# A planned attention and MoE kernel: the first job's scores moved behind half of its gate spreads, and other margins in the planner

## The chip, the cores and the metric

The kernel runs on one core of one Trainium2 chip. The metric is the device time of one execution in microseconds; the times before are the median of three runs. A profile is one execution recorded by the hardware profiler; it has a span (first to last instruction) and a time of its own.

## What is computed

Three stages follow each other. The first is a gated linear attention in the manner of an mLSTM (4 batches, 8 heads, 768 steps, head size 40), which the reference writes as a loop over time:

```python
m_new = np.maximum(f_gate[:, :, t] + m, i_gate[:, :, t])
f_stab = np.exp(f_gate[:, :, t] + m - m_new)
i_stab = np.exp(i_gate[:, :, t] - m_new)
C = f_stab[..., None, None] * C + i_stab[..., None, None] * np.einsum('bhd,bhe->bhde', vt, kt)
n = f_stab[:, :, None] * n + i_stab[:, :, None] * kt
h_tilde = np.einsum('bhde,bhe->bhd', C, qt)
denom = np.maximum(np.abs(np.einsum('bhd,bhd->bh', n, qt)[:, :, None]), 1.0)
y[:, :, t] = sigmoid(o_gate[:, :, t]) * h_tilde / denom
```

Its output, 3072 tokens of 320 numbers, goes through two layers of the form `g(x @ w_in) @ w_out` with 2048 inner features: `g(h) = h - tanh(h)` in the first, and in the second `h` above 1, 0 below -1 and `(h + 1)**2 / 4` between.

## The kernel before

The time axis is cut into 6 chunks of 128 steps. A **job** is one chunk of one batch, 24 in all (`job`, line 408). Four jobs make a **block** of 512 tokens, and each of the two layers runs over 6 blocks and, in a block, over 16 slices `f` of 128 inner features: `step` computes `h = x @ w_in` (lines 651 and 661), `activate` the function on ScalarE (ACT) and VectorE (DVE), `second` adds `gh @ w_out` into four PSUM banks `a` (line 713), two slices later (`LAG`). In the first layer the jobs of block k+1 are threaded between the slices of block k.

A job goes this way. The gates' decays are spread over partitions: for the first four jobs by matmuls against columns of the identity (`t_f`, line 453, two halves of four heads, each in its own `h` bank), later by loads `fb` from DRAM. DVE scans them into `d` (line 462), once for each half. TensorE makes the scores `t_s` (line 475, later 493 with split inputs from line 490), DVE multiplies them into `d` (line 497), TensorE makes `t_n` (lines 524, 533), then follow ACT line 540, DVE lines 541 and 542, GpSimd (POOL) line 556, DVE line 558 (the product `x`), and the transposes `t_x` (line 562). From these ACT and DVE make the split inputs of the next block (lines 612 to 617). The state update is `t_c` (line 569) with ACT lines 577, 581 and DVE line 586. The gates themselves come from `gates` (line 342): exponentials on ACT (line 369), then transposes `t_i` on TensorE (line 374).

Beside that the weights, which come as 64-bit floats, are loaded, converted on ACT and DVE (`conv64`, lines 322 to 326) and split (`split_w`, line 335). Results of a block of the first layer are transposed on DVE (line 724) and stored to `xr_d` by four DMAs. All loads and stores but one stand in SyncE's queue (SP), line 287, which issues them in order.

The order of all this isn't written by hand. `Plan` (line 76) records every operation with an engine, an estimated duration and a priority, simulates the engines, and emits each engine's instructions in the order of the planned starts. A result counts as available `NEAR` ns after its end for another engine, `FAR` for TensorE, and an own `margin` later where one is set. The priority of job `n` of a later block is `st = NF * (k - 1) + NF * (n - BLK0[k]) / BLK[k] - AHEAD`, in units of slices, and its loads have `st - LOADS`. Up to the end of the first slice TensorE's planned gaps are filled with matmuls on zeros (`filler`, line 804), a whole number of them for each gap, plus `P.more[o]` ahead of an operation `o`.

Of the kernel before, what the change touches and what calls it, by code (L numbers as in the profile page):

```python
# [18 lines left out]
L = 128  # L19
# [23 lines left out]

LOAD = [-90, -89, -88, -86]
JOB0, JOBD, JOBS = -30, 4, 1.0
AHEAD, LOADS = 6, 3
GROUPS = [(0, 2)] + [(c, c + 1) for c in range(2, NC)]
GATES = [-95, 12, 28, 44, 58]
DECAYS = [-94, 13, 29, 45, 59]
# [26 lines left out]
class Plan:  # L76
# [1 line left out]

    NEAR, FAR, PE_OUT = 60.0, 130.0, 170.0
    DMA_IN, DMA_OUT, DMA_ISSUE = 1400.0, 900.0, 370.0
    BACKLOG = 4000.0
    PATIENCE = 150.0
    FILL, HEAD, COLD = 0.75, 1.0, 4000.0

    def __init__(self):
        self.ops, self.tags, self.last, self.read = [], {}, {}, {}
        self.warm, self.end_warm, self.filler, self.gate, self.more = True, None, None, None, {}

    def buf(self, pool, shape, dtype, tag, name, cap=1):
        b = Buf(pool, shape, dtype, tag, name, cap)
# [4 lines left out]
    def op(self, eng, ns, prio, fn, r=(), w=(), out=None, lock=False):  # L97
        o = Op()
        o.eng, o.ns, o.prio, o.fn, o.seq, o.out = eng, ns, prio, fn, len(self.ops), out
        o.allocs, o.preds, o.succs = [], set(), []  # L100
        o.bufs, o.fill, o.lock, o.margin = [], 0, lock, 0.0
        key = lambda x: x if isinstance(x, tuple) else (x, None)

        for x in map(key, r):
            if x in self.last:
                o.preds.add(self.last[x])
            self.read.setdefault(x, []).append(o)
        for x in map(key, w):
            if x in self.last:
                o.preds.add(self.last[x])  # L110
            o.preds.update(self.read.pop(x, ()))
            self.last[x] = o
        o.preds.discard(o)
        for b in {key(x)[0] for x in (*r, *w)}:
            if isinstance(b, Buf):
                b.users.append(o)
                o.bufs.append(b)
        if any(b.place[0].startswith("late_") for b in o.bufs):
            o.preds.add(self.gate)
        self.ops.append(o)  # L120
        return o

    def schedule(self):
# [32 lines left out]
        while done < len(self.ops):  # L156
# [24 lines left out]
            if o.out is not None:  # L181
                dma = max(dma, t + self.DMA_IN) + o.out
                o.end = dma + self.DMA_OUT + o.margin
                free[o.eng] = t + self.DMA_ISSUE
            else:
                free[o.eng] = t + o.ns
                o.end = t + o.ns + (self.PE_OUT if o.eng == "PE" else 0.0)
            for b in o.bufs:
                b.left -= 1
                b.end = max(b.end, o.end)  # L190
# [2 lines left out]
            for s in o.succs:  # L193
# [5 lines left out]
                if not s.left:  # L199
                    ready[s.eng].append(s)  # L200
            done += 1
        self.ops.sort(key=lambda o: (o.start, o.seq))

    def issue(self):
# [28 lines left out]
def mlstm_moe_moe(ctx: ExitStack, tc: tile.TileContext, ig, fg, qk, qk3, q3, nat, w1, w2, cst, out):  # L233
# [64 lines left out]
    def load64(layer, f, prio):  # L298
# [3 lines left out]
        else:  # L302
            t = abuf("w64", [128, 8 * WC], U8, 2)
        raw_w[layer, f] = t
        load(prio, lambda: t[:, 0:8 * WC - 3], lambda: (w1, w2)[layer][f].bitcast(U8)[:, 3:8 * WC],
             704, w=[t], rows=5629, margin=6000.0 if layer else 0.0)

    def conv64(layer, f, prio):

# [98 lines left out]
    def job(n, at, ld):  # L408
# [10 lines left out]
            for u in range(2):  # L419
                load(ld, lambda u=u: qs[u].t, lambda u=u: qk3[b, c - STACK // B, u], 480, w=[qs[u]])  # L420
        nt = wbuf(3, [128, 2 * DM + H * E1], F32, "nat0") if n == 0 else abuf("nat", [128, 2 * DM + H * E1], F32, 3)
        load(ld, lambda: nt.t, lambda: nat[b, c * L:(c + 1) * L], 484, w=[(nt, 0), (nt, 1), (nt, 2)], rows=3872, margin=1200 if n >= 8 else 0.0)
        kc = group[c]
        f = {}
        if n >= FIRST:
            for u in range(2):
                ft = abuf("fb", [128, HU, L], F32, 2)
                load(ld + 0.5, lambda ft=ft: ft.t.rearrange("p h t -> p (h t)"), lambda u=u: fr_d[
                    c, b * H + u * HU:b * H + (u + 1) * HU].rearrange("h t -> (h t)").unsqueeze(0).to_broadcast([128, HU * L]),
                    256, r=[("fr_d", kc)], w=[ft], rows=512, margin=1200 if n >= 8 else 0.0)  # L430
                f[u] = lambda ft=ft: ft.t.rearrange("p h t -> p (h t)"), ft
        if c > 0:
            g = abuf("gb", [120, 3, L], F32, 2)
            for i in range(3):
                m = 3 if i < 2 else 2
                load(ld + 0.7, lambda i=i, m=m: g[i * D:(i + 1) * D, 0:m, :], lambda i=i, m=m: gr_d[
                    c, b * H:(b + 1) * H].unsqueeze(0)[:, i:H:3].to_broadcast([D, m, L]),
                    20 * m, r=[("gr_d", kc)], w=[(g, i)], rows=512, margin=1200 if n >= 8 else 0.0)
            G = [(g, i) for i in range(3)]
            q = abuf("q3", [120, 3, L], F32, 1)  # L440
            load(ld + 0.8, lambda: q.t, lambda: q3[b, c], 180, w=[(q, 0), (q, 1)], rows=1536, margin=1200 if n >= 8 else 0.0)


        dk = {}
        d0 = wbuf(6 + n % 2, [128, 1024], F32, "d0") if n < FIRST else None
        wc = abuf("wc", [128, H], F32, 2)
        for u in range(2):
            p = at(0) if u == 0 else at(1)
            if n < FIRST:
                ft = jbank(n, "f", "t_f")  # L450
                for h in range(HU):
                    r = b * H + u * HU + h
                    op("PE", 2 * pe(L, 128, 2), p, lambda h=h, r=r, ft=ft: nc.tensor.matmul(  # L453
                        ft[:, h * L:(h + 1) * L], ident[:, r:r + 1].to_broadcast([128, 128]),
                        gt[0][0][:, 0:L], start=True, stop=True), [(gt[0][0], 0), (gt[0][0], "z", 32), (gt[0][0], "z", 64), "cs"], [ft])
                f[u] = lambda ft=ft: ft.t, ft
            if d0 is None:
                d = abuf("d", [128, 512], F32, 3)
# [19 lines left out]

        if n < STACK:
            o = op("PE", 455 + 2 * HU * 111, at(1), scores, [(qt, 0), (qt, 1)], [sp[0], sp[1]])  # L480
            if n == 1:
                P.more[o] = 3
        else:
# [460 lines left out]
```

## Time and profile before

| | us |
|---|---|
| three runs | 808.71, 808.29, 806.84 |
| median | 808.29 |
| profiled execution, own time | 807.17 |
| its span | 805.4 |
| TensorE busy in the span | 798.4 |
| DVE, ACT, POOL busy | 566.4, 426.3, 145.1 |

The granted TensorE clock is 1.0 of full speed in all 40 slices of the page. A timeline row gives the start, the length, the engine, the line, the operation and what it writes and reads, the shape and the count; in brackets stands the engine's idle time ahead of it and what ended it. Ends of matmuls are modelled, so a short wait can hide in the length of the matmul before it. `PE` is TensorE, and `SPq` the queue of SyncE.

### The profile page before, as it was taken

The numbers are of one execution on the slowest core, as the hardware profiler recorded it, in microseconds if no ns is written. First come the engines' busy times: TensorE is split into PE (matmuls) and PEld (weight loads), VectorE is DVE, ScalarE is ACT, GpSimd is POOL, SyncE is SP. The second block draws the span as 40 slices with busy tenths as digits, with TensorE's granted clock in tenths as the row PEclk, the third lists the DMA queues.
The fourth block names the chain that finished last, engine by engine and source line by source line (L and its number), as shares of the span: only waits on it lengthen the run. The fifth ranks groups of instructions, "written<-read, shape, count | busy, mean of one in ns | idle before, by whom it ended". The sixth has DMA issues, their size and how long they took to land.

```text
span 805.4 us, 15259 instructions
## 1 busy us (share of the span) xinstructions
PE 798.4 (99%) x6029; PEld 693.3 (86%) x6029; DVE 566.4 (70%) x924; ACT 426.3 (53%) x810; POOL 145.1 (18%) x146
## 2 busy tenths in 40 slices
PE   9999999999999999999999999999999999999998
PEld 7666888888988989898899898888889889898887
DVE  7999998988887897887466674645546465564644
ACT  4966876566586657554455543534435344342533
POOL 3142233213225234332100200200200101000000
PEclk9999999999999999999999999999999999999999
DMA  8979356676668576771543310100100000000000
GB/s 281 326 225 308 104 178 178 180 246 188 174 172 260 163 213 165 228 217 64 145 133 91 93 34 1 40 33 1 47 26 1 33 1 1 33 1 1 34 1 33
DMA packets 47619, 93.66 MB, mean 116 GB/s; under 512 B 4700, under 2 KB 25020, under 8 KB 47548
## 3 DMA queue, kind: packets, MB, share of 16 engines
q1 hardware_dynamic: 47500, 92.66, 38.8%
q8 instruction: 47, 0.77, 0.4%
q14 instruction: 24, 0.20, 0.1%
q10 hardware_dynamic: 48, 0.03, 0.0%
HBM read 78.88 MB, written 13.80 MB: 115 GB/s over the span
## 4 chain that ended last, share of the span: by engine, by line
PE 95%; DVE 2%; DMA 1%; SPq 0%; issue 0%; ACT 0%; POOL 0%; POOLq 0%; DVEq 0%; ACTq 0%
PE a L713 41%; PE h L661 38%; PE h L651 3%; PE t_n L533 2%; PE h L640 2%; PE t_n L524 2%; PE t_s L475 1%; PE t_c L569 1%; PE t_s L493 1%; PE t_x L562 1%; PE t_f L453 1%; PE spare L807 1%; DMA nat<-in_nat_dram 1%; DVE d L462 1%; SPq L287 0%
## 5 line engine op out<-in xcount | busy, mean ns | idle before, releaser
L661 PE MATMUL h<-x,w 128*128 128x512 f32 x1376 | 340.6, 396 | 0.0
L713 PE MATMUL a<-w,gh 128*128 128x320 f32 x1472 | 328.4, 310 | 0.0
L661 PEld LDWEIGHTS h<-x,w 128*128 128x128 f32 x1376 | 251.6, 188 | 55.2 <-issue 6.9
L713 PEld LDWEIGHTS a<-w,gh 128*128 128x128 f32 x1472 | 248.7, 188 | 8.0 <-ACT ob L736 1.8
L713 PE MATMUL a<-w,gl 128*128 128x320 f32 x736 | 228.2, 311 | 0.0
L684 DVE TENSOR_SCALAR g<-h 128x512 f32<-128x512 f32 x96 | 63.6, 684 | 115.9 <-PE h L661 115.9
L686 ACT ACTIVATE g<-g,half 128x512 f32<-128x512 f32 x96 | 66.9, 721 | 136.2 <-DVE g L684 135.7
L713 PEld LDWEIGHTS a<-w,gl 128*128 128x128 f32 x736 | 138.1, 188 | 0.4
L688 DVE TENSOR_TENSOR g<-h,g 128x512 f32<-128x512 f32 x96 | 64.6, 692 | 27.7 <-ACT g L686 26.9
L692 ACT CAST gh<-g 128x512 fp32r<-128x512 f32 x96 | 59.5, 623 | 43.1 <-DVE g L688 39.8
L680 DVE TENSOR_TENSOR h<-h,g 128x512 f32<-128x512 f32 x88 | 60.9, 693 | 26.8 <-ACT g L679 26.3
L679 ACT ACTIVATE g<-h 128x512 f32<-128x512 f32 x88 | 52.6, 598 | 46.6 <-PE h L661 46.2
L693 DVE TENSOR_TENSOR gl<-h,gh 128x512 fp32r<-128x512 f32 x88 | 59.9, 684 | 20.1 <-ACT gh L692 19.1
L777 POOL TENSOR_TENSOR x<-xl,x 128x512 fp32r<-128x512 f32 x18 | 24.8, 1398 | 271.2 <-ACT x L768 270.7
L692 ACT CAST gh<-h 128x512 fp32r<-128x512 f32 x88 | 51.4, 585 | 40.5 <-DVE h L680 25.4
L693 DVE TENSOR_TENSOR gl<-g,gh 128x512 fp32r<-128x512 f32 x96 | 61.9, 686 | 2.9
L462 DVE TENSOR_TENSOR_SCAN d<-fb,scan_id 128x512 f32<-128x512 f32 x40 | 52.8, 1326 | 2.0 <-DMA fb<-fr_d 1.8
L490 POOL TENSOR_TENSOR xf<-qkraw,xf 120x1024 fp32r<-120x1024 f32 x12 | 29.6, 2467 | 79.5 <-ACT xf L488 48.3
L488 ACT ACTIVATE xf<-qkraw,cs 120x512 fp32r<-120x512 f32 x48 | 32.7, 718 | 15.7 <-PE t_s L493 10.7
L497 DVE TENSOR_TENSOR d<-t_s,d 128x512 f32<-128x512 f32 x48 | 31.8, 680 | 4.6 <-PE t_s L493 2.4
L556 POOL TENSOR_TENSOR nat<-nat,dn 128x320 f32<-128x320 f32 x23 | 21.7, 944 | 69.6 <-DVE dn L542 67.7
L322 ACT ACTIVATE cvb<-w,half 128x704 bf16<-128x704 int8 x32 | 29.8, 932 | 2.1 <-DVE w L324 2.1
(105 smaller groups left out, 754.0 us busy)
## 6 DMA issues: line engine op xcount, KB each, us to landing
w<-in_w_dram SPq DMA_DIRECT2D x32, 703.6 KB
nat<-in_nat_dram SPq DMA_DIRECT2D x24, 484.0 KB
qkraw<-in_qk_dram SPq DMA_DIRECT2D x24, 480.0 KB
fb<-fr_d SPq DMA_DIRECT2D x40, 256.0 KB
w_d<-w SPq DMA_DIRECT2D x16, 352.0 KB
w<-w_d SPq DMA_DIRECT2D x16, 352.0 KB
qkraw<-in_qk_dram SPq DMA_DIRECT2D x24, 160.0 KB
xr_d<-xo SPq DMA_DIRECT2D x24, 160.0 KB
```

The source lines that it names most:

```text
L462: op("DVE", dve(1024), p, lambda o=dk[u][0], i=f[u][0]: nc.vector.tensor_tensor_scan(out=o(), data0=i(), data1=scan_id, initial=0.0, op0=A ...
L488: op("ACT", act(512, 1), at(u - 1), lambda raw=raw, t=t, z=z, cols=cols: nc.scalar.activation(t[:, cols], raw[:, cols], AF.Copy, scale=cs[ ...
L497: op("DVE", dve(512), at(2 + u), lambda p=sp[u], d=dk[u][0]: nc.vector.tensor_tensor(out=d(), in0=p.t, in1=d(), op=ALU.mult), [sp[u], dk[u ...
L661: op("PE", pe(n), prio, lambda i=i, c=c, s=s: nc.tensor.matmul(p[:, :n], w[:, c:c + 128], x[:, s, :n], start=(i == 0 and not layer), stop= ...
L679: op("ACT", act(n), prio + 0.5 - FFN, lambda: nc.scalar.activation(t[:, :n], p[:, :n], AF.Tanh), [p], [t])
L680: op("DVE", dve(n), prio + 0.5 - FFN, lambda: nc.vector.tensor_tensor(out=p[:, :n], in0=p[:, :n], in1=t[:, :n], op=ALU.subtract), [p, t], [p])
L684: op("DVE", dve(n), prio + 0.5 - FFN, lambda: nc.vector.tensor_scalar(t[:, :n], p[:, :n], -1.0, 1.0, op0=ALU.max, op1=ALU.min), [p], [t])
L686: op("ACT", act(n, 1), prio + 0.5 - FFN, lambda: nc.scalar.activation(t[:, :n], t[:, :n], AF.Square, bias=half[:, 0:1], scale=0.5), [t, "h ...
L688: op("DVE", dve(n), prio + 0.5 - FFN, lambda: nc.vector.tensor_tensor(out=t[:, :n], in0=p[:, :n], in1=t[:, :n], op=ALU.max), [p, t], [t])
L692: op("ACT", act(n), prio + 1 - FFN, lambda: nc.scalar.copy(gh[:, :n], y[:, :n]), [y], [gh])
L693: op("DVE", dve(n), prio + 1 - FFN, lambda: nc.vector.tensor_tensor(out=gl[:, :n], in0=y[:, :n], in1=gh[:, :n].bitcast(F32), op=ALU.subtra ...
L713: op("PE", pe(DM) if gl is not None else 2 * pe(DM, 128, 2), prio, lambda A=A, r=r, a=a, c=c, i=i, dt=dt: nc.tensor.matmul(A[:, 0:DM], a[: ...
```

## The change

Four things are changed.

1. The scores of job 0 get three more fillers ahead of them, and are then put behind the first half of the job's `t_f` matmuls: after the planning, if they are planned to start before the last `t_f` of the first half, their start is set just behind it, and the fillers planned ahead of them go to the TensorE operation that followed them.
2. `NEAR` goes from 60 to 100 ns, and every DVE operation with a priority above -9 gets a tenth of its duration as a margin.
3. `AHEAD` goes from 6 to 5 and `LOADS` from 3 to 2.
4. The margin of the second layer's weight loads goes from 6000 to 5000 ns.

```diff
-AHEAD, LOADS = 6, 3
+AHEAD, LOADS = 5, 2
...
-    NEAR, FAR, PE_OUT = 60.0, 130.0, 170.0
+    NEAR, FAR, PE_OUT = 100.0, 130.0, 170.0
...
+    LATE = {"POOL": 0.0, "DVE": 0.1, "ACT": 0.0}
...
-        o.bufs, o.fill, o.lock, o.margin = [], 0, lock, 0.0
+        o.bufs, o.fill, o.lock = [], 0, lock
+        o.margin = self.LATE.get(eng, 0.0) * ns if prio > -9 else 0.0
...
-                o.end = t + o.ns + (self.PE_OUT if o.eng == "PE" else 0.0)
+                o.end = t + o.ns + o.margin + (self.PE_OUT if o.eng == "PE" else 0.0)
...
+        for o, first in self.behind:
+            if o.start <= first.start:
+                after = min((x for x in self.ops if x.eng == o.eng and (x.start, x.seq) > (o.start, o.seq)), key=lambda x: (x.start, x.seq))
+                after.fill, o.fill = after.fill + o.fill, 0
+                o.start = first.start + 0.5
...
-             704, w=[t], rows=5629, margin=6000.0 if layer else 0.0)
+             704, w=[t], rows=5629, margin=5000.0 if layer else 0.0)
...
-                    op("PE", 2 * pe(L, 128, 2), p, lambda h=h, r=r, ft=ft: nc.tensor.matmul(
+                    o = op("PE", 2 * pe(L, 128, 2), p, lambda h=h, r=r, ft=ft: nc.tensor.matmul(
...
+                    bc.append(o)
...
             o = op("PE", 455 + 2 * HU * 111, at(1), scores, [(qt, 0), (qt, 1)], [sp[0], sp[1]])
+            if n == 0:
+                P.more[o] = 3
+                P.behind.append((o, bc[HU - 1]))
```

Line numbers in the new kernel are higher, by 7 at line 287 and by 11 at line 533. TensorE's queue at the start, before; each of the ten fillers is one pair of a weight load and a `spare` matmul, of which the last pair stands here:

```order
L807 LDWEIGHTS gh
L807 MATMUL spare<-gh 128x512
L475 MATMUL t_s<-qkraw 128x128 x8
L374 MATMUL t_i<-cs,gate_92 128x32 x2
L453 MATMUL t_f<-gate_90,cs 128x128 x8
L807 LDWEIGHTS gh
```

And now, behind thirteen fillers:

```order
L818 LDWEIGHTS gh
L818 MATMUL spare<-gh 128x512
L381 MATMUL t_i<-cs,gate_92 128x32 x2
L460 MATMUL t_f<-gate_90,cs 128x128 x4
L483 MATMUL t_s<-qkraw 128x128 x8
L460 MATMUL t_f<-gate_90,cs 128x128 x4
L818 LDWEIGHTS gh
```

The scores have moved from ahead of `t_i` to between the halves of `t_f`. The rest of TensorE's queue up to the first slice is the same but for two places: a filler ahead of the second `t_x` is gone, and one `t_s` stands ahead of a `t_c` instead of within it.

SP's queue at the end of the first block, before (the four `xr_d` are the stores of its result; the two `fb` between and behind them are job 10's, the two ahead of `q_1550` job 9's):

```order
L287 DMA qkraw<-in_qk_dram 40x1024 x2
L287 DMA fb<-fr_d 128x512 x2
L287 DMA q_1550<-in_q_dram 120x384
L287 DMA xr_d<-xo 32x10x128 x3
L287 DMA fb<-fr_d 128x512
L287 DMA xr_d<-xo 32x10x128
L287 DMA nat<-in_nat_dram 128x968
L287 DMA fb<-fr_d 128x512
```

And now:

```order
L294 DMA fb<-fr_d 128x512 x2
L294 DMA qkraw<-in_qk_dram 40x1024 x2
L294 DMA q_1571<-in_q_dram 120x384
L294 DMA fr<-in_fg_dram 32x128
L294 DMA ig<-in_ig_dram 32x128
L294 DMA fb<-fr_d 128x512 x2
L294 DMA nat<-in_nat_dram 128x968
L294 DMA xr_d<-xo 32x10x128 x4
```

Job 10's two loads and the `nat` load of job 11 have moved ahead of all four stores.

DVE's queue in job 17, from the maximum of line 541 to the product `x` of line 558, before (`gl` and `h` are the first layer's activation, `w` the conversion of a second-layer weight, `d<-fb` the scans of jobs 18 and 19):

```order
L541 TENSOR_SCALAR dn<-t_n 128x8
L542 RECIPROCAL dn<-dn 128x8
L693 TENSOR_TENSOR gl<-h,gh 128x512
L462 SCALAR_TENSOR_TENSOR d<-fb,scan_id 128x512
L326 SCALAR_TENSOR_TENSOR w_3339<-w_3199,w_3339 128x704
L462 SCALAR_TENSOR_TENSOR d<-fb,scan_id 128x512
L680 TENSOR_TENSOR h<-h,g 128x512
L586 SCALAR_TENSOR_TENSOR C<-C,gb,t_c 120x123 x2
L693 TENSOR_TENSOR gl<-h,gh 128x512
L680 TENSOR_TENSOR h<-h,g 128x512
L558 TENSOR_TENSOR x<-t_n,nat 128x320
```

And now:

```order
L552 TENSOR_SCALAR dn<-t_n 128x8
L553 RECIPROCAL dn<-dn 128x8
L470 SCALAR_TENSOR_TENSOR d<-fb,scan_id 128x512
L597 SCALAR_TENSOR_TENSOR C<-C,gb,t_c 120x123
L691 TENSOR_TENSOR h<-h,g 128x512
L597 SCALAR_TENSOR_TENSOR C<-C,gb,t_c 120x123
L569 TENSOR_TENSOR x<-t_n,nat 128x320
```

One scan, the weight conversion and one pair of activation instructions have moved to other places in the queue, and on TensorE the job's `t_x` stands nearer to its `t_n`: 8 `a` and 16 `h` matmuls lie between them, where 41 and 16 lay before.

## Rows read from the trace of the kernel before

**Rows 1.** The page's first part: busy us, share of the span, instructions.

```profile
PE 798.4 (99%) x6029; PEld 693.3 (86%) x6029; DVE 566.4 (70%) x924; ACT 426.3 (53%) x810; POOL 145.1 (18%) x146
```

**Rows 2.** TensorE's waits: waiter, releaser, us in total, times, longest.

```profile
PE t_x L562 <- DVE x L558: 0.9, 1, 0.9
PE t_n L524 <- POOL nat L504: 0.7, 1, 0.7
PE t_x L562 <- DVE x L553: 0.5, 1, 0.5
PE t_i L374 <- DVE x L617: 0.2, 1, 0.2
```

**Rows 3.** Windows: length, busy PE, PEld, DVE, ACT, POOL; clock, DMA share, GB/s.

```profile
31.10:112.40 81.30, 81.30 (x646) 59.07 (x645) 75.15 (x120) 58.91 (x114) 20.48 (x20) 1.00 0.67 209
452.00:802.00 350.00, 350.00 (x1971) 309.39 (x1969) 196.22 (x311) 144.85 (x230) 20.93 (x15) 1.00 0.06 19
```

**Rows 4.** Timeline of TensorE in the head.

```profile
1.32 3.74 PE L807 MATMUL spare<-gh 128*128 128x512 bf16 x10 [1.32 <-POOL gh L810]
4.99 1.61 PE L475 MATMUL t_s<-qkraw 40*128 40x128 f32 x16
6.53 0.30 PE L374 MATMUL t_i<-cs,gate 32*128 32x32 f32 x2
6.76 2.05 PE L453 MATMUL t_f<-gate,cs 128*128 128x128 f32 x16
8.65 0.81 PE L807 MATMUL spare<-gh 128*128 128x512 bf16 x3
9.39 1.16 PE L475 MATMUL t_s<-qkraw 40*128 40x128 f32 x16
...
21.61 0.38 PE L807 MATMUL spare<-gh 128*128 128x512 bf16 x1
...
31.11 7.99 PE L651 MATMUL h<-xf,wf 128*128 128x512 f32 x18
```

**Rows 5.** Timeline of DVE and of ACT in the head.

```profile
8.03 2.34 DVE L462 TENSOR_TENSOR_SCAN d<-t_f,scan_id 128x512 f32<-128x512 f32 x2 [0.93 <-PE t_f L453]
...
11.68 2.34 DVE L462 TENSOR_TENSOR_SCAN d<-t_f,scan_id 128x512 f32<-128x512 f32 x2
...
4.63 0.75 ACT L369 ACTIVATE gate<-gate 32x256 f32<-32x256 f32 x2 [2.16 <-DVE gate L364]
```

**Rows 6.** Timeline of SP's queue at the first block's end.

```profile
122.82 2.98 SPq L287 DMA_DIRECT2D xr_d<-xo  x3
125.90 0.40 SPq L287 DMA_DIRECT2D fb<-fr_d  x1
```

**Rows 7.** Timelines of DVE and TensorE behind those loads.

```profile
130.51 1.23 DVE L462 TENSOR_TENSOR_SCAN d<-fb,scan_id 128x512 f32<-128x512 f32 x1 [1.76 <-DMA fb<-fr_d]
...
133.22 0.87 PE L524 MATMUL t_n<-C,q 120*128 120x123 f32 x6 [0.69 <-POOL nat L504]
```

**Rows 8.** Timelines of DVE and TensorE in job 17.

```profile
284.85 2.45 DVE L326 SCALAR_TENSOR_TENSOR w<-w,w 128x704 int32<-128x704 int32 x1
...
291.50 0.52 PE L562 MATMUL t_x<-cs,x 128*128 128x128 f32 x3 [0.90 <-DVE x L558]
```

**Rows 9.** Line 326 (ns: shortest, median, longest), and a meeting of DVE and POOL.

```profile
L326 DVE SCALAR_TENSOR_TENSOR w<-w,w x24: 840/888/3005, 50.7 to 366.1; 128x704 int32<-128x704 int32 x24
...
222.81 3.00 DVE L326 SCALAR_TENSOR_TENSOR w<-w,w 128x704 int32<-128x704 int32 x1
...
222.68 2.39 POOL L490 TENSOR_TENSOR xf<-qkraw,xf 120x1024 fp32r<-120x1024 f32 x1 [10.58 <-PE t_n L524]
```

**Rows 10.** Timelines of TensorE and ACT ahead of the second block.

```profile
108.22 0.49 PE L562 MATMUL t_x<-cs,x 128*128 128x128 f32 x3
...
109.06 0.38 ACT L612 CAST x<-t_x 128x256 fp32r<-128x256 f32 x1
...
109.95 0.94 ACT L322 ACTIVATE w<-w,half 128x704 f32<-128x704 int8 x1
```

More of the change, by code (lines that the diff above doesn't have):

```diff
@@ L88, in __init__ @@
         self.ops, self.tags, self.last, self.read = [], {}, {}, {}
-        self.warm, self.end_warm, self.filler, self.gate, self.more = True, None, None, None, {}
+        self.warm, self.end_warm, self.filler, self.gate, self.more, self.behind = True, None, None, None, {}, []
     def buf(self, pool, shape, dtype, tag, name, cap=1):
@@ L421, in job @@
         nt = wbuf(3, [128, 2 * DM + H * E1], F32, "nat0") if n == 0 else abuf("nat", [128, 2 * DM + H * E1], F32, 3)
-        load(ld, lambda: nt.t, lambda: nat[b, c * L:(c + 1) * L], 484, w=[(nt, 0), (nt, 1), (nt, 2)], rows=3872, margin=1200 if n >= 8 else 0.0)
+        load(ld, lambda: nt.t, lambda: nat[b, c * L:(c + 1) * L], 484, w=[(nt, 0), (nt, 1), (nt, 2)], rows=3872, margin=1200.0 if n >= 8 else 0.0)
         kc = group[c]
@@ L429, in job @@
                     c, b * H + u * HU:b * H + (u + 1) * HU].rearrange("h t -> (h t)").unsqueeze(0).to_broadcast([128, HU * L]),
-                    256, r=[("fr_d", kc)], w=[ft], rows=512, margin=1200 if n >= 8 else 0.0)
+                    256, r=[("fr_d", kc)], w=[ft], rows=512, margin=1200.0 if n >= 8 else 0.0)
                 f[u] = lambda ft=ft: ft.t.rearrange("p h t -> p (h t)"), ft
@@ L437, in job @@
                     c, b * H:(b + 1) * H].unsqueeze(0)[:, i:H:3].to_broadcast([D, m, L]),
-                    20 * m, r=[("gr_d", kc)], w=[(g, i)], rows=512, margin=1200 if n >= 8 else 0.0)
+                    20 * m, r=[("gr_d", kc)], w=[(g, i)], rows=512, margin=1200.0 if n >= 8 else 0.0)
             G = [(g, i) for i in range(3)]
             q = abuf("q3", [120, 3, L], F32, 1)
-            load(ld + 0.8, lambda: q.t, lambda: q3[b, c], 180, w=[(q, 0), (q, 1)], rows=1536, margin=1200 if n >= 8 else 0.0)
-        dk = {}
+            load(ld + 0.8, lambda: q.t, lambda: q3[b, c], 180, w=[(q, 0), (q, 1)], rows=1536, margin=1200.0 if n >= 8 else 0.0)
+        dk, bc = {}, []
         d0 = wbuf(6 + n % 2, [128, 1024], F32, "d0") if n < FIRST else None
```

## The prediction

> **What bounds the kernel now.** I read the page's first part, then TensorE's list of waits, then the windows by stage, then the timelines around each wait. TensorE is counted busy for 798.4 us, 99% of the profiled span [rows 1], and the list of its waits holds, besides the start, four entries that sum to 2.3 us [rows 2]. So nearly all of the time is TensorE's own work. The matmuls of the reference's three stages are the same in number before and after; only fillers (matmuls on zeros, line 807) are added, two in all. From 452 to 802 us TensorE is busy for 350.0 of 350.0 us [rows 3]; nothing can be won there. What can move is the head (up to the first `h` matmul at 31.1 us [rows 4]), and the waits between 31 and 400 us, where the attention jobs are threaded between the matmuls of the first MoE layer. There VectorE (DVE) is nearly as full: 75.15 of 81.3 us between 31.1 and 112.4 us [rows 3].
>
> **Part 1: the first job's scores.** Before, ten fillers run from 1.32 us, then the scores (`t_s`) at 4.99, the gate transposes (`t_i`) at 6.53, the gate spreads (`t_f`) at 6.76, the next fillers at 8.65 us [rows 4]. These scores take 1.61 us where the second job's take 1.16 [rows 4]. The gates' exponentials on ScalarE end at 4.63 + 0.75 = 5.38 us [rows 5], so `t_i` waits only for TensorE's queue. Three fillers more cost what three cost elsewhere, 9.39 - 8.65 = 0.74 us, so `t_i` starts near 4.99 + 0.74 = 5.73, 0.8 us earlier. It takes 0.23 us, and half of the spread gates half of 8.65 - 6.76, 0.95 us: done at 6.91 instead of 7.71, and the first scan on DVE moves from 8.03 [rows 5] to about 7.2 us. But the second scan needs the other half, and that now stands behind the scores: 6.91 + 1.1 + 0.95 = 8.96 us, 0.3 us later than the 8.65 of before. With the 0.32 us that lay between the first half's end (7.71) and its scan (8.03), the second scan starts at 9.28; before, it started half of 2.34 us after 8.03, at 9.20. So the early first scan only opens a gap on DVE, and its second end is 0.1 us late; job 1's spread gates come 0.1 to 0.3 us late, and DVE's scan at 11.68 us [rows 5] follows them. What gives this back is the one filler that the new order no longer has ahead of the second `t_x`: it took about 0.2 us at 21.61 [rows 4]. 0.1 late and 0.2 back: **head -0.1 us**, between -0.35 (none of the delay reaches the end) and +0.3 (all of it does, and the filler was covering a wait).
>
> **Part 2: the planner's margins.** `NEAR` 100 for 60, a tenth of DVE's time as a margin, jobs and loads one step later (`AHEAD`, `LOADS`): nothing of this costs time by itself, it only re-orders the queues from 31 us on. I priced the four waits by what now stands at their places.
> - The wait of 0.7 us of `t_n` [rows 2]. SP's queue stood at the `xr_d` stores from 122.82 for 2.98 us and issued the gates `fb` of job 10 only at 125.90 [rows 6]; DVE then sat idle for 1.76 us until they landed at 130.5, the multiply that frees `t_n`'s bank was late behind that scan, and TensorE waited 0.69 us before 133.22 [rows 7]. In the new order both `fb` loads and `nat` stand ahead of all four `xr_d` stores. The load needs its buffer (a scan of job 9, which comes just before these stores in either order), so it can leave up to 2.98 us earlier, which is more than the 1.76. **-0.7 us**, between -0.9 (idle time is counted from a modelled end) and 0.
> - The wait of 0.9 us of `t_x`. Between the reciprocal and the product `x` of job 17 DVE had nine instructions, among them two scans and line 326, which took 2.45 us beside GpSimd's work; `t_x` then waited 0.90 us before 291.50 [rows 8]. Now there are four, one scan and no line 326. **-0.9 us**, between -1.1 and 0.
> - The `t_i` wait of 0.2 us behind line 617 [rows 2]: in the new order 3.4 us of matmuls (worked out from the spacing of like matmuls in the timeline) stand between that job's `t_x` and `t_i`, before 1.8. **-0.2 us**, between -0.3 and 0.
> - New waits. The closest place that I find is the start of the second block: between the last `t_x` of job 7 and the first `h` that needs it stood nine `a` matmuls, now six, about 0.9 us, and the `h` on the low part and `t_i` follow at once. The path is `t_x` (0.49), a cast on ScalarE (0.38), then two on DVE; in the new order a weight conversion of 0.94 us stands ahead of that cast on ScalarE [rows 10]. So 0 to 0.9 us; I take **+0.2**, since the three-step path at its shortest just fits. All other job hand-offs keep distances of the kind that were free of waits before.
>
> Sum: -0.1 - 0.7 - 0.9 - 0.2 + 0.2 = **-1.7 us**. The profiled execution took 807.17 us (span 805.4), so its like after is 805.5; the median of the three runs is 808.29 (806.84 to 808.71), 1.1 above the profiled one, and the same step gives **806.6 us**. About 0.2%, 1.6 us, is what a measurement of this kernel can tell from no change, so the forecast lies just past that edge.
>
> **Rivals.** (A) *The waits only change place.* The four were accidents of an order that is now another, and a new order has its own. For it: the queues of TensorE, DVE and SP differ nearly everywhere between 40 and 390 us, and planned distances are as tight as before. Against it: the margins that were raised are those towards DVE, and two of the three larger waits were DVE's. If the sum of waits stays at 2.3 us, the two fillers cost up to 0.4 us and the head gives nothing: 808.3 + 0.0 to + 0.4, so **808.4 us**.
> (B) *DVE and GpSimd meet more often, and the kernel is slower.* Place: the conversions of line 326 and the scans between 31 and 390 us, with GpSimd's products of jobs beside them. Price: line 326 takes 0.89 us in the median and up to 3.0 us, and that longest one began at 222.81, 0.13 us after GpSimd's line 490 of 2.39 us [rows 9]; the one of 2.45 us, 1.6 us too long, ended in the wait of 0.9 us [rows 8]. Two more such meetings ahead of a hand-off, with no old wait gone, give 808.3 + 2 x 0.9 = **810.1 us**. It decides from the point where TensorE's waits after the head pass 3.9 us. For it: jobs shifted against conversions mean new neighbours. Against it: the planner keeps these pairs apart in either version, and the job 17 meeting lost its line 326.
> The Trainium skill, SBUF — State Buffer, section Who interferes with whom, states that a DVE instruction with two SBUF inputs contends with a GpSimd instruction that reads SBUF, and that whoever comes second blocks fully. By that rule line 326 would have waited out line 490 (2.39 - 0.13 = 2.26 us) and then worked 0.89: 3.15 us, against 3.00 in the trace, which agrees to 0.15.
> (C) *The move at the start does what its words say and no more.* This is part 1's bound, +0.3 us, and changes no verdict.
>
> **How the numbers follow.** Forecast 0.50 (806.6, its own range 805.6 to 807.5 by the bounds above; six tenths of it count as faster by over 0.2%); rival A with C 0.36 (within 0.2%, but for a quarter, since runs of one kernel lie up to 1.9 us apart here); rival B 0.14. Faster: 0.5 x 0.6 + 0.36 x 0.25 = 0.39; slower: 0.14 x 0.85 + 0.36 x 0.05 = 0.14; same: the rest, 0.47. Range: all old waits gone and the head at its bound is -0.35 - 0.9 - 1.1 - 0.3 = -2.65, 805.6, less 0.8 for the spread of runs: 804.8. Above, rival A at 808.4 with half that spread and a first part of rival B: 809.5. That leaves most of rival B and little else outside.
>
> **What would show it.** Right: the first scan on DVE near 7.2 us and the second near 9.3; the first `h` at 31.1 +- 0.3; no DVE wait on `fb` near 130 us; no `t_x` wait on DVE near 291; TensorE's waits after the head under 1 us. Wrong: a wait of `h`, `t_i` or `t_s` of over 0.5 us near 112 us; line 326 or a scan of over 2 us with a TensorE wait behind it; a first `h` later than 31.5 us; any wait in the last 350 us, where the stores of a block's result now have less matmul work ahead of the bank's next use.

## The result: 0.6% slower

The changed kernel takes 812.22 us (median of 7 runs, 810.45 to 815.65), the kernel before beside it 807.62 (7 runs, 806.84 to 808.94): 1.006 times the time, interval 1.0038 to 1.0082. The forecast was 806.6, in a range up to 809.5. It was wrong in its sign.

The profiled execution of the new kernel is the longest of its seven (815.65 us), so its parts sum to more than the medians differ by. Its first part and TensorE's waits (waiter, releaser, us in total, times, longest), to be read against [rows 1] and [rows 2]:

```profile
span 813.9 us, 15314 instructions
...
PE 802.2 (99%) x6027; PEld 696.0 (86%) x6031; DVE 572.6 (70%) x924; ACT 426.4 (52%) x812; POOL 154.8 (19%) x146
```

```profile
PE t_x L573 <- DVE x L569: 3.7, 3, 2.3
...
PE t_s L483 <- issue: 1.0, 1, 1.0
PE t_n L535 <- issue: 0.7, 1, 0.7
PE t_x L573 <- DVE x L564: 0.5, 1, 0.5
PE t_n L544 <- issue: 0.5, 1, 0.5
```

The wait of `t_n` on `nat` and that of `t_i` are gone, as forecast. But `t_x` now waits for 3.7 us in three places where it waited 0.9 in one. GpSimd, with the same 146 instructions, is busy for 154.8 us instead of 145.1: some of them took longer. TensorE in the head, against [rows 4]:

```profile
1.32 5.58 PE L818 MATMUL spare<-gh 128*128 128x512 bf16 x13 [1.32 <-POOL gh L821]
6.82 0.30 PE L381 MATMUL t_i<-cs,gate 32*128 32x32 f32 x2
7.06 1.16 PE L460 MATMUL t_f<-gate,cs 128*128 128x128 f32 x8
8.14 1.16 PE L483 MATMUL t_s<-qkraw 40*128 40x128 f32 x16
9.24 1.16 PE L460 MATMUL t_f<-gate,cs 128*128 128x128 f32 x8
...
32.27 1.24 PE L818 MATMUL spare<-gh 128*128 128x512 bf16 x5 [0.16 <-issue]
...
35.11 1.12 PE L662 MATMUL h<-xf,wf 128*128 128x512 f32 x2
```

The span is 8.5 us longer. The first `h` comes at 35.11 us instead of 31.11: 4.0 us are lost in the head. From the first `h` to the end the new kernel needs 813.9 - 35.11 = 778.8 us, the old one 805.4 - 31.11 = 774.3: 4.5 us are lost behind it. Of these the waits explain 3.7 + 0.7 new, less the 1.8 old ones behind the head, 2.6 us. TensorE's clock explains most of the rest. It is granted at half (0.50, 1.2 of 2.4 GHz) in two short stretches of this execution (columns: stretch, length, busy PE, PEld, DVE, ACT, POOL with counts, clock, DMA share, GB/s):

```profile
27.10:30.50 3.40, 3.18 (x15) 2.73 (x16) 3.27 (x5) 1.12 (x5) 0.11 (x1) 0.50 0.92 372
153.40:156.80 3.40, 3.40 (x16) 2.46 (x16) 2.89 (x5) 0.53 (x2) 0.00 (x0) 0.50 0.93 347
```

The first follows the 1.0 us pause of `t_s` in the head, the second the 2.3 us wait of `t_x` at 152.90. From that `t_x` to the next job's second `t_n` (line 544) it is 6.87 us here, and 5.41 in a second profile of the same kernel (experiment 4) where the clock stayed at 1.00: 1.5 us for the second stretch. From the end of the pause to the first `h` it is 9.08 us here and 7.42 there: 1.7 us for the first, which lie within the 4.0 us of the head. The same pause and the same wait stand in that second profile too, so neither brings the clock down every time.

### The profile page after: what moved, and what is told of

Read it like the earlier page. It is cut to its first block, busy times and chain, and to the rows that moved or that the text cites. A ratio compares the mean times of both kernels' runs of the same rounds, so it can differ in the third digit from the quotient of the medians.

```text
span 813.9 us, 15314 instructions
## 1 busy us (share of the span) xinstructions
PE 802.2 (99%) x6027; PEld 696.0 (86%) x6031; DVE 572.6 (70%) x924; ACT 426.4 (52%) x812; POOL 154.8 (19%) x146
## 4 chain that ended last, share of the span: by engine, by line
PE 94%; DVE 2%; issue 1%; ACT 1%; POOL 0%; DVEq 0%; ACTq 0%; POOLq 0%
PE a L724 41%; PE h L672 38%; PE h L662 3%; PE t_n L544 2%; PE h L651 2%; PE t_s L483 2%; PE t_n L535 2%; PE t_c L580 1%; PE t_s L504 1%; PE t_x L573 1%; PE spare L818 1%; PE t_f L460 1%; DVE h L691 0%; DVE w L333 0%; DVE d L470 0%
## 5 line engine op out<-in xcount | busy, mean ns | idle before, releaser
L695 DVE TENSOR_SCALAR g<-h 128x512 f32<-128x512 f32 x96 | 66.1, 689 | 122.4 <-PE h L672 122.4
L697 ACT ACTIVATE g<-g,half 128x512 f32<-128x512 f32 x96 | 69.5, 724 | 154.4 <-DVE g L695 154.0
L704 DVE TENSOR_TENSOR gl<-g,gh 128x512 fp32r<-128x512 f32 x96 | 65.8, 729 | 0.7 <-ACT gh L703 0.7
L470 DVE TENSOR_TENSOR_SCAN d<-fb,scan_id 128x512 f32<-128x512 f32 x40 | 58.0, 1464 | 0.1
L525 POOL TENSOR_TENSOR q<-q,gb 120x256 f32<-120x256 f32 x20 | 21.3, 1065 | 75.1 <-DMA q<-in_q_dram 59.6
```

The lines of the kernel that those rows point to most:

```text
L470: op("DVE", dve(1024), p, lambda o=dk[u][0], i=f[u][0]: nc.vector.tensor_tensor_scan(out=o(), data0=i(), data1=scan_id, initial=0.0, op0=A ...
L695: op("DVE", dve(n), prio + 0.5 - FFN, lambda: nc.vector.tensor_scalar(t[:, :n], p[:, :n], -1.0, 1.0, op0=ALU.max, op1=ALU.min), [p], [t])
L697: op("ACT", act(n, 1), prio + 0.5 - FFN, lambda: nc.scalar.activation(t[:, :n], t[:, :n], AF.Square, bias=half[:, 0:1], scale=0.5), [t, "h ...
L704: op("DVE", dve(n), prio + 1 - FFN, lambda: nc.vector.tensor_tensor(out=gl[:, :n], in0=y[:, :n], in1=gh[:, :n].bitcast(F32), op=ALU.subtra ...
```

## Where the 2.3 us wait comes from

TensorE, DVE and GpSimd around the long wait, job 9, in the new kernel:

```profile
152.90 0.52 PE L573 MATMUL t_x<-cs,x 128*128 128x128 f32 x3 [2.28 <-DVE x L569]
```

```profile
145.45 0.87 DVE L342 TENSOR_TENSOR w<-wf,w 128x704 fp32r<-128x704 f32 x1
146.25 0.87 DVE L331 TENSOR_TENSOR w<-w,cvb 128x704 int32<-128x704 f32 x1
147.16 4.09 DVE L333 SCALAR_TENSOR_TENSOR w<-w,w 128x704 int32<-128x704 int32 x1
151.17 0.69 DVE L691 TENSOR_TENSOR h<-h,g 128x512 f32<-128x512 f32 x1
151.77 0.58 DVE L597 SCALAR_TENSOR_TENSOR C<-C,gb,t_c 120x123 f32<-120x123 f32 x2
152.28 0.48 DVE L569 TENSOR_TENSOR x<-t_n,nat 128x320 f32<-128x320 f32 x1
```

```profile
145.38 2.07 POOL L527 TENSOR_TENSOR q<-q,gb 80x128 f32<-80x128 f32 x1
147.41 0.72 POOL L567 TENSOR_TENSOR nat<-nat,dn 128x320 f32<-128x320 f32 x1
148.09 2.40 POOL L501 TENSOR_TENSOR xf<-qkraw,xf 120x1024 fp32r<-120x1024 f32 x1
```

The weight conversion (now line 333, before 326) took 4.09 us where its median is 0.89. It began while GpSimd's product `q` ran, and stood until GpSimd's third product ended at 148.09 + 2.40 = 150.49; its end, 151.25, is 0.76 us after that. Behind it in DVE's order stood the activation, `C` and the product `x`, for which `t_x` waits. GpSimd's `q` in turn took 2.07 us instead of the 0.46 that line 527 takes at 293.91; lines 342 and 331 ran on DVE beside it.

The other conversions of this form show the same. The 17 profiles of this document hold 544 of them. The 392 with no GpSimd product beside them took 0.86 to 0.91 us. The 76 that took over 1.2 us all began while a GpSimd product ran, and ended 0.74 to 0.77 us after the end of one: of that same product in 50 cases, and in 26 of one or two later ones that had followed it without a gap and got ahead of the conversion. In 24 cases such a follower did not get ahead; what decides this stays open. In the trace of before the conversion of 3.00 us [rows 9] had met one product of 2.39 us. The one of 2.45 us [rows 8], by which I had priced a meeting, had let two products pass, but short ones (GpSimd, before):

```profile
283.80 1.38 POOL L516 TENSOR_TENSOR q<-q,gb 80x128 f32<-80x128 f32 x1
285.14 0.72 POOL L556 TENSOR_TENSOR nat<-nat,dn 128x320 f32<-128x320 f32 x1
285.83 0.72 POOL L510 TENSOR_TENSOR nat<-nat,wc 128x320 f32<-128x320 f32 x1
```

In the new order the last of the three takes 2.40 us.

## The experiments

A ratio is to the kernel before, run beside it on the same chip, with its 95% interval. In the diffs `marks` is a dictionary of recorded operations, and a move sets an operation's start after the planning, so that it changes place on its engine and nothing else moves: `P.ahead` puts it `d` ns ahead of another operation's start (behind it where `d` is negative), `P.behind` behind another.

**1 to 4: the head and the planner apart.** Experiment 1 leaves out the head's move, experiment 2 has it alone, experiment 3 has it without the three fillers, experiment 4 is the changed kernel again.

```diff
 (1)        if n == 0:
-                P.more[o] = 3
-                P.behind.append((o, bc[HU - 1]))
 (2)
-AHEAD, LOADS = 5, 2
+AHEAD, LOADS = 6, 3
-    NEAR, FAR, PE_OUT = 100.0, 130.0, 170.0
+    NEAR, FAR, PE_OUT = 60.0, 130.0, 170.0
-    LATE = {"POOL": 0.0, "DVE": 0.1, "ACT": 0.0}
+    LATE = {"POOL": 0.0, "DVE": 0.0, "ACT": 0.0}
-margin=5000.0 if layer else 0.0
+margin=6000.0 if layer else 0.0
 (3) as (2), and
-                P.more[o] = 3
```

> The new planner numbers (margins, AHEAD, LOADS, weight loads) without the move of the first job's scores and its three fillers. Theory P (half and half): in the profile after, 4.0 of the 8.5 us by which its span is longer had come by the first h, the rest behind it, from waits of t_x on VectorE after long instructions next to GpSimd. Then this kernel loses the part behind the head alone: 809.0 to 811.0 us, about +2.5 against the kernel before, with the first h near 31.0 us and the t_x wait of over 2 us still there. Rival H (all of it starts in the head: the later start shifts everything against the loads and so makes the later meetings): 807 to 808 us, and the long VectorE instruction near 147 us is gone. Rival Q (the planner alone): 811.5 to 813 us.

> The kernel before with the move of the first job's scores and its three fillers alone; everything else in the old order. Theory P: TensorE's queue is later by about 1.6 us at the first job's t_n and never wins that back, so 809.0 to 810.5 us, with the first h at 32.5 to 33.5 us and the waits behind the head as before. Rival H: 811 to 813 us, new long waits between 31 and 400 us although the order there is the old one. Rival Q: 807.3 to 808.3 us.

> The kernel before with the scores behind the first half of the spread gates, but without the three more fillers. Theory P: what costs is that the fillers run at half of the clock (0.43 us each, where I had taken 0.25) and stand ahead of t_i; without them t_i starts by 5.8 us and the second scan by 9.5, so the time is that of the kernel before within 0.6 us, 807.2 to 808.6. A rival, that the scores between the halves are what costs: 808.8 to 810 us, with the second scan on VectorE later than 10 us.

> The changed kernel itself once more, on the same chip as the parts, with a second profile. Theory P: 811.5 to 813 us; the waits of t_x on the product x of over 2 us and of over 1 us come back at the same places, since the order is the same; the two dips of the granted clock are at other places or missing, since the runs of the changed kernel spread over 5 us. If waits and dips both come back at the same places, the dips are part of the order's price; if the long waits don't come back, they are an accident of one execution.

| | us | before | ratio |
|---|---|---|---|
| 1 planner alone | 810.90 | 807.29 | 1.0056 (1.0042 to 1.0070) |
| 2 head alone | 808.24 | 807.29 | 1.0012 (1.0003 to 1.0021) |
| 3 head without fillers | 806.86 | 807.29 | 0.9998 (0.9989 to 1.0007) |
| 4 the changed kernel | 812.01 | 807.29 | 1.0061 (1.0048 to 1.0074) |

The two parts add up to the whole: the planner's numbers cost 3.6 us by the medians, the head's move 0.9, of which nothing is left without its three fillers. Experiment 1 has the time that theory P gave it, though its first `h` came at 31.95 us and not near 31.0. Experiment 2 lies under theory P's 809 us, where rival Q had it. Its profile has the first `h` at 32.93 us, as theory P had it, but in an execution 0.9 us above the median. Of the 4.0 us that the profile of the changed kernel shows in the head, 1.7 are its stretch at half clock, which no other profile has there; in experiment 4 the first `h` comes at 33.27. The waits of `t_x` came back at the same instructions in 1 and 4 (3.7 us in three, longest 2.3); the stretch at half clock behind the longest came back in 1 (149.7 to 153.0 us) and not in 4.

**5 to 7: the waits taken away, first try.** Experiment 5 puts job 9's `x` ahead of the long conversion, on the base of experiment 1; experiment 6 puts job 17's maximum on ScalarE ahead of a gate exponential and a conversion; experiment 7 has both, with the head of experiment 3.

```diff
 (5)
+    P.ahead += [(marks["q", 10], marks["w", 1, 1], 3), (marks["o", 9], marks["w", 1, 1], 2), (marks["x", 9], marks["w", 1, 1], 1)]
 (6)
+    P.behind += [(marks["exp", 4, True], marks["abs", 17]), (marks["cv", 1, 12, -1.0], marks["abs", 17])]
```

> The planner part without the head move (810.9 us), with one VectorE instruction at another place: job 9's product x ahead of the weight conversion (line 333) instead of four places later, behind it. Theory M (the meeting on the port of VectorE and GpSimd is what t_x waits for): the conversion still takes over 3 us, but the 2.3 us wait of t_x near 150 us is gone and with it the granted clock's fall behind that wait: 808.0 to 809.0 us. Rival N (the wait moves on: the conversion now holds up the activation behind it, and an a or h matmul waits instead): 810 to 811 us, with a wait of over 1 us within 10 us of the place. Rival C (the clock falls there for another reason): the runs still spread to above 812 us.

> The planner part without the head move (810.9 us), with two ScalarE instructions in another order: job 17's t_n maximum (ACTIVATE t_n) ahead of a gate exponential, its table load and a weight conversion, 2.5 us of work, instead of behind them. Theory M2: the product x of job 17 is then 1.3 us or more earlier, and the 1.27 us wait of t_x near 295 us is gone: 809.3 to 810.0 us. Rival N2 (VectorE's scan and the activations ahead of x end no earlier, x is late anyway): 810.5 to 811.2 us with at least 0.8 us of that wait left.

> The changed kernel with both moves above, and with the scores of the first job behind half of its spread gates but without the three more fillers. If the losses add (head 0 to -0.4, wait 2.3 with its clock, wait 1.3): 806.2 to 807.3 us, equal to the kernel before or just under it. If there are further losses in the new order than these two waits: 808 to 809 us. If the waits move on: 809 to 811.

Experiment 5: 810.09 us, ratio 1.0039 (1.0027 to 1.0051). The wait of 2.3 us became one of 1.6, of another matmul, as rival N had it:

```profile
PE a L731 <- ACT gh L710: 1.6, 1, 1.6
PE t_x L580 <- DVE x L575: 1.4, 2, 1.3
```

The conversion, now 2.68 us, still stood ahead of the activation whose result `a` needs. Experiment 6: 811.97 us, 1.0053 (1.0041 to 1.0065), no gain, and the 1.27 us wait stayed, as rival N2 had it. Experiment 7: 809.95 us, 1.0037 (1.0024 to 1.0050), with the 1.6 and the 1.3 us waits: the waits had moved on. What held job 17's `x` is seen in the changed kernel's ScalarE and DVE rows:

```profile
293.05 1.28 ACT L376 ACT_TABLE_LOAD   x1
294.35 0.31 ACT L376 ACTIVATE ig<-ig 32x128 f32<-32x128 f32 x1
294.56 0.91 ACT L329 ACTIVATE cvb<-w,half 128x704 bf16<-128x704 int8 x1
295.37 0.15 ACT L551 ACTIVATE t_n<-t_n 128x8 f32<-128x8 f32 x1
```

```profile
295.56 0.17 DVE L552 TENSOR_SCALAR dn<-t_n 128x8 f32<-128x8 f32 x1 [3.57 <-ACT t_n L551]
...
296.99 0.34 DVE L597 SCALAR_TENSOR_TENSOR C<-C,gb,t_c 120x123 f32<-120x123 f32 x1
297.50 0.70 DVE L691 TENSOR_TENSOR h<-h,g 128x512 f32<-128x512 f32 x1 [0.17 <-ACT g L690]
298.11 0.34 DVE L597 SCALAR_TENSOR_TENSOR C<-C,gb,t_c 120x123 f32<-120x123 f32 x1
298.36 0.48 DVE L569 TENSOR_TENSOR x<-t_n,nat 128x320 f32<-128x320 f32 x1
```

DVE was idle for 3.57 us, waiting for the maximum of `t_n`, which stood on ScalarE behind a table load, the exponential of a gate and a conversion. With the maximum ahead of them, `C` and the activation `h` on DVE still waited for ScalarE behind the same three, and `x` behind those.

**8 to 10: the planner's numbers one by one.** On the base of experiment 1: 8 has only `AHEAD, LOADS = 5, 2`, 9 only `NEAR` 100 and the tenth of DVE's time, 10 only the weight loads' 5000; the other numbers as before.

> Of the planner's numbers only AHEAD and LOADS (5 and 2 for 6 and 3); NEAR, the tenth of VectorE's time and the weight loads' margin as before. Theory O (the loss is that of an order, not of a number: whichever number changes, VectorE and GpSimd drift into other meetings): another order with other waits, 808 to 811 us, with at least one VectorE instruction of over 2.5 us at a place where neither of the two kernels has one. Rival A (the later jobs are what costs): 810 to 811.5 us with the 4.1 us conversion near 145 us again. Rival L (the margins are what costs): 806.5 to 808 us.

> Of the planner's numbers only NEAR (100 for 60) and the tenth of VectorE's time as a margin; AHEAD, LOADS and the weight loads' margin as before. Theory O (every new order has waits of its own): 807.5 to 810 us, with at least one new wait of over 0.7 us between 31 and 400 us. Rival L (more margin towards VectorE gives fewer waits, as I had argued): 806.0 to 807.2 us, waits behind the head under 1.2 us in sum.

> Of the planner's numbers only the margin of the second layer's weight loads (5000 for 6000). Theory O: 807 to 809 us, another order between about 110 and 390 us, other waits. Rival S (a number as small as that changes a few rows and no time): 806.8 to 807.6 us with the four old waits at their places.

| | us | before | ratio | TensorE's largest waits behind the head |
|---|---|---|---|---|
| 8 AHEAD, LOADS | 813.70 | 807.24 | 1.0085 (1.0068 to 1.0102) | `a` 4.8, `t_x` 1.1 |
| 9 NEAR, tenth | 807.84 | 807.41 | 1.0006 (0.9995 to 1.0017) | `t_n` 0.6, `t_n` 0.2 |
| 10 weight loads | 810.35 | 807.41 | 1.0037 (1.0024 to 1.0051) | `t_x` 3.5 in four, `t_s` 0.8 |

They don't add: 6.5 + 0.4 + 2.9 by the medians, against 3.6 for the three together. Experiments 8 and 10 have orders with waits of their own, which neither of the two kernels has, as theory O had it, but both cost more than it gave them (at most 811 and 809 us). Experiment 9 changes nothing that can be measured; its 0.6 us wait is job 4's `t_n`, which the changed kernel has too, and the new wait of over 0.7 us that theory O wanted did not come. In experiment 8 it is not a meeting of DVE and GpSimd that costs most. A late load shows how far a wait travels (ScalarE, DVE and TensorE):

```profile
121.14 1.28 ACT L516 ACT_TABLE_LOAD   x1 [1.65 <-DMA nat<-in_nat_dram]
```

```profile
123.41 0.69 DVE L701 TENSOR_TENSOR gl<-h,gh 128x512 fp32r<-128x512 f32 x1 [2.01 <-ACT gh L700]
...
127.35 1.85 DVE L333 SCALAR_TENSOR_TENSOR w<-w,w 128x704 int32<-128x704 int32 x1
129.12 0.68 DVE L701 TENSOR_TENSOR gl<-h,gh 128x512 fp32r<-128x512 f32 x1
129.72 0.90 DVE L732 STREAM_TRANSPOSE xo<-a 128x320 f32<-128x320 f32 x2
```

```profile
PE a L721 <- DVE xo L732: 4.8, 1, 4.8
```

ScalarE waits 1.65 us for a job's `nat` load, DVE 2.01 us for ScalarE, and the transposes that free the banks of `a` stand last in DVE's order, behind a conversion that a meeting with GpSimd makes 1.0 us longer. The granted clock was 0.50 from 129.2 to 135.9 us: it fell within that wait, which ended at 130.37.

**11 and 12: second try, and the old order with its waits removed.** Experiment 11 is 5, with job 17's exponential and conversion behind ScalarE's scalings of `t_c`. Experiment 12 is experiment 3 with the two waits taken out that the forecast had priced at 0.9 and 0.7.

```diff
 (11)
+    P.behind += [(marks["exp", 4, True], marks["tc", 17]), (marks["cv", 1, 12, -1.0], marks["tc", 17])]
 (12)
+    P.ahead += [(marks["o", 17], marks["sc", 19, 0], 2), (marks["x", 17], marks["sc", 19, 0], 1), (marks["fb", 10, 0], marks["xr", 0, 0], 1)]
```

> The planner part without the head move (810.9 us), with job 9's x ahead of the weight conversion, as in the run with that move alone (810.1), and in job 17 the gate exponential, its table load and the conversion behind ScalarE's five scalings of t_c as well as behind the maximum. The first trial left these scalings behind them, and the product x behind VectorE's first C, which waits for them. If that is why it did nothing: C starts near 290.7 us instead of 293.3, x is some 1.5 us earlier, the t_x wait near 295 falls from 1.27 to under 0.3, and the time is 808.6 to 809.2 us. If the scan and the activation ahead of x set its time as well: 809.6 to 810.3 us and 0.8 us or more of the wait stays.

> The kernel before in its old order, with three moves that the forecast had priced: the first job's scores behind half of the spread gates without more fillers (0 to -0.4 us), job 17's product x ahead of six VectorE instructions (wait of 0.9), and the first fb load of job 10 ahead of three stores of xr_d (wait of 0.7). If the prices of the single waits were right and nothing else moves: 805.2 to 806.2 us, with no t_n wait near 133 and no t_x wait near 291. If waits only move on: 806.6 to 807.5 us.

Experiment 11: 811.47 us, 1.0048 (1.0034 to 1.0062), above both of its ranges. The 1.3 us wait was still there: `C` now came at 291.20, but the activation ahead of `x` waited 2.33 us for a tanh behind the same exponential; a wait of `a`, 0.7 us at 125.80, was new. Experiment 12: 807.10 us, 0.9995 (0.9987 to 1.0004). Both old waits were gone from TensorE's list, and a new one of 0.7 us stood 3 us behind the place of the second (line 511 is the scores, 640 the second low part that DVE makes from `t_x`):

```profile
PE t_s L511 <- DVE x L640: 0.7, 1, 0.7
```

**13 to 15: the conversion behind everything that is waited for.** Experiment 13 moves only the conversion, behind the activation, `C`, `x` and `gl` (a load and a store that depend on it are set behind it and keep their places in SP's queue). Experiment 14 has also the two moves of experiment 11 in job 17, and `x` ahead of its first `C`. Experiment 15 is 14 with the head of experiment 3.

```diff
 (13)
+    P.ahead += [(marks["w", 1, 1], marks["gl", 22.0], -1), (marks["ld", 1, 3], marks["gl", 22.0], -2), (marks["st", 1], marks["gl", 22.0], -3)]
 (14) as (13), the line of (11), and
+    P.ahead += [(marks["o", 17], marks["C", 17, 0], 2), (marks["x", 17], marks["C", 17, 0], 1)]
```

> The planner part without the head move (810.9 us), with the weight conversion of line 333 that took 4.1 us moved back by five VectorE instructions, behind the activation h, both parts of C, the product x of job 9 and gl. Theory M (the meeting of this conversion with GpSimd's three products is the cause of the 2.3 us wait): VectorE is free when these five come, the conversion meets GpSimd later or not at all, neither t_x nor a waits over 0.5 us near 150 us, and the time is 808.3 to 809.0 us. Rival N (the activation and C come no earlier, or the shifted conversion blocks the next job): 809.7 to 810.7 us, with 1 us or more of waits between 145 and 165 us.

> As the run before, and in job 17 ScalarE's gate exponential with its table load and conversion behind the five scalings of t_c, and the product x ahead of VectorE's first C, so that it waits for GpSimd's product alone. If the two waits are the planner part's loss: no t_x wait over 0.3 us near 295 us, 807.0 to 807.8 us, the kernel before within 0.5. If a loss of another kind is left (the spread of the runs, the first second t_n near 48 us): 808 to 809 us.

> As the run before, with the first job's scores behind half of its spread gates, without the three more fillers. If the parts add, 0 to 0.5 us under the run before: 806.6 to 807.5 us, no measurable gain over the kernel before; for a gain the waits of job 4's t_n and of t_x at the end of the head would have to go too.

| | us | before | ratio |
|---|---|---|---|
| 13 | 808.31 | 807.86 | 1.0004 (0.9993 to 1.0015) |
| 14 | 807.47 | 807.86 | 0.9995 (0.9985 to 1.0005) |
| 15 | 807.96 | 807.86 | 0.9998 (0.9990 to 1.0007) |

One instruction moved back by five places takes the planner's part from 1.0056 to 1.0004. DVE in experiment 13, at the same place:

```profile
145.72 0.70 DVE L701 TENSOR_TENSOR h<-h,g 128x512 f32<-128x512 f32 x1 [1.25 <-ACT g L700]
146.32 0.59 DVE L606 SCALAR_TENSOR_TENSOR C<-C,gb,t_c 120x123 f32<-120x123 f32 x2
146.83 0.48 DVE L576 TENSOR_TENSOR x<-t_n,nat 128x320 f32<-128x320 f32 x1
147.23 0.68 DVE L714 TENSOR_TENSOR gl<-h,gh 128x512 fp32r<-128x512 f32 x1
147.82 0.88 DVE L338 SCALAR_TENSOR_TENSOR w<-w,w 128x704 int32<-128x704 int32 x1
```

GpSimd's three products are those of the changed kernel, without a gap between them; the last:

```profile
145.44 2.41 POOL L505 TENSOR_TENSOR xf<-qkraw,xf 120x1024 fp32r<-120x1024 f32 x1
```

The conversion takes 0.88 us, and neither `t_x` nor `a` waits there, as theory M had it. Its gain by the medians, 810.90 - 807.29 less 808.31 - 807.86, is 3.2 us, more than the 2.3 us of the wait; the stretch at half clock, which followed that wait in two of the four profiles that have it, is the likely rest. One such stretch takes 0.002 off an execution's mean granted clock; that mean is 0.998 in five of the six executions of experiment 1, and 0.999 or 1.000 in all twelve of experiment 13. Experiment 14 also removes the wait of job 17, but `t_s` then waits 0.5 us at 294.75. Experiment 15, forecast at or under experiment 14, came 0.5 us above it, within the intervals. No version beats the kernel before by more than the intervals.

## Why the prediction was wrong, step by step

**Part 1, three fillers for 0.74 us: mis-sized.** Thirteen took 5.58 us, 0.43 each, where five at 32.27 us took 0.25 each. I priced them by three later ones (0.25 each), though the row that stood in the same place said otherwise: ten in 3.74 us [rows 4]. So `t_i` came at 6.82 us instead of 5.73 and the scans at 8.32 and 10.43 instead of 7.2 and 9.28. In all 17 profiles the fillers of this first group start 0.40 to 0.43 us apart up to a point that differs between executions, and 0.21 to 0.23 behind it (last section). In the trace of before that point is 4.2 us, so the ten fillers of [rows 4] already run partly at the later pace; here it is 6.6 us, when all thirteen have started. The three more thus cost some 1.3 of the 1.84 us between 5.58 and 3.74, and that the pace changed later in this execution makes the rest. The Trainium skill, TensorE: Matmul & The Clock Gate, section "Wait — 56ns, not 53.3ns?", gives 426.7 ns from start to start for matmuls of 512 columns at the lower clock; the 0.42 to 0.43 us of nearly all of these agree. The head's term, -0.1 with an upper bound of +0.3, measured +0.9 by the medians of experiment 2 (0.2 to 1.7 by its interval), and experiment 3 shows that the fillers alone make it.

**The wait of 0.7 us of `t_n`: right.** Both loads of job 10 left ahead of the stores, and in the new trace DVE scans without idle time:

```profile
128.81 2.61 SPq L294 DMA_DIRECT2D fb<-fr_d  x2
132.10 0.33 SPq L294 DMA_DIRECT2D nat<-in_nat_dram  x1
132.52 2.39 SPq L294 DMA_DIRECT2D xr_d<-xo  x4
```

The `t_i` wait of 0.2 us is gone too. But another `t_n`, job 4's at 52.82, now waits 0.7 us, and I had no term for it.

**The wait of 0.9 us of `t_x`: wrong.** It is the same job 17 that waits now, for 1.27 us, and for ScalarE's queue rather than for a meeting of DVE and GpSimd. I counted the DVE instructions between the reciprocal and `x` and found fewer. I did not ask when the first of them could start (it waited 3.57 us for ScalarE), nor what it meant that the new order had also taken 33 `a` matmuls away between `t_n` and `t_x`: from the end of `t_n` to `t_x` it was 11.3 us before and is 6.9 now.

**New waits, +0.2: the main error.** I looked for them at one place, the start of the second block, where none came, and took the other hand-offs for safe since their distances on TensorE looked alike. In job 9 the distance was long enough (9.0 us of TensorE's work, 4.7 before), and DVE was still late, through the 4.09 us conversion. What I held against rival B, that the planner keeps DVE and GpSimd apart, is the step that failed: it keeps their planned times apart, and nothing keeps the engines to these times. Where the sum had +0.2 us, the profile has 4.4 us of waits behind the head (2.3 in job 9, 1.3 in job 17, 0.7 in job 4), and 1.5 us of lower clock behind the first of them. In the plan GpSimd's second `q` product started when the conversion ended; on the chip GpSimd took it up 1.8 us ahead of the conversion. Rival B had the right mechanism for the largest wait (line 326 beside a job's GpSimd products, in job 9). The 4.4 us of waits also pass the 3.9 from which it was to decide, but only 2.3 of them come from such a meeting, so that this mark came out right is in part luck. Its price of 0.9 us for a meeting was too low: it was the wait that a conversion 1.6 us too long had left in job 17, and this one was 3.2 us too long; and it had no term for the clock.

The page of the Trainium skill that the prediction weighed, SBUF — State Buffer, section Who interferes with whom, holds in its main point: whoever comes second waits. Its other half is that a DVE instruction with at most one SBUF input, outside the two-port modes that the page names, does not contend with GpSimd. Experiment 13 agrees: DVE's `h`, `x` and `gl`, each with one input in PSUM and one in SBUF, took 0.70, 0.48 and 0.68 us though GpSimd was working until 147.85 us; `h` and `x` take 0.69 and 0.48 in the changed kernel, behind GpSimd's products. What the trace adds is that a waiting DVE instruction let two later GpSimd instructions pass; the trace of before had that too, in the conversion of 2.45 us, and I had not looked at what it waited for.

**What was right.** TensorE stayed the bound, and the last 350 us were not touched; the window that answers to the second of [rows 3]:

```profile
460.50:810.50 350.00, 350.00 (x1971) 309.32 (x1969) 198.62 (x311) 142.09 (x230) 21.89 (x15) 1.00 0.06 19
```

TensorE is busy for 350.00 of 350.00 us as before: all that was lost lies ahead of it.

## What to carry to other kernels

Where a planner keeps two engines apart only in planned time, a new order must be priced by its meetings: list each pair of instructions that can block each other within a microsecond or two, and ask what stands behind the loser on its engine. The loser waits at least for the instruction that it met, and at most, here, for two more that followed that one without a gap. A wait that an order has lost is worth less than its length, since the next hand-off is often just behind it (experiment 12), and a wait on TensorE can cost more than its length when its clock falls behind it. Price fillers from the row at their own place, and time such changes in many runs: here each of three small numbers moved the kernel by 0 to 0.85%.

## What had not been expected of the hardware

The same ten fillers at the start took 3.67 us in experiment 5 and 4.45 us in experiment 11:

```profile
1.32 3.67 PE L825 MATMUL spare<-gh 128*128 128x512 bf16 x10 [1.32 <-POOL gh L828]
```

```profile
1.32 4.45 PE L829 MATMUL spare<-gh 128*128 128x512 bf16 x10 [1.32 <-POOL gh L832]
```

TensorE's speed in its first microseconds thus differs between executions of the same work; the first `h` came at 30.79 us in the one and at 32.29 in the other. The traces' records of the granted clock tell the two apart. They begin, at 1.00, at 4.05 us in experiment 5 and at 7.05 us, behind all ten fillers, in experiment 11; in the 17 profiles they begin between 3.99 and 7.33 us. The fillers of the first group start 0.40 to 0.43 us apart ahead of that point and 0.21 to 0.23 behind it; the one step across it lies between. What was granted ahead of it is not recorded (a window there reads 1.00), and what sets the point stays open. In the head TensorE also pauses within one group of matmuls, for nothing that the profile shows (1.0 us within `t_s` in the changed kernel, 0.9 in experiment 4, 0.7 in experiment 1); what it waits for there stays open.
